# A fused linear attention and MLP kernel: one more block of 512 tokens, and k projections as full-array products

## The chip, the core and the metric

The kernel runs on one core of a Trainium2 chip. A core has five engines that run side by side and meet only at semaphores: PE (TensorE, the matrix multiplier, which writes to PSUM), DVE (VectorE, elementwise work and reductions), ACT (ScalarE, activation functions and copies), POOL (GpSimd) and SP (SyncE, which here only issues transfers). PEld in the profile is the loading of a matmul's stationary operand. The metric is the device time of one execution in microseconds (us); lower is better.

## What is computed

Linear attention over 8 batches of 576 tokens with 8 heads of 64, followed by a two-layer perceptron over all 4608 tokens:

```python
def phi(x):
    proj = np.einsum('bhsd,df->bhsf', x, w_phi)
    proj = proj - np.max(np.abs(proj), axis=-1, keepdims=True)
    return np.concatenate([np.exp(proj), np.exp(-proj)], axis=-1)

q_p, k_p = phi(q), phi(k)
kv = np.einsum('bhsf,bhsd->bhfd', k_p, v)
z = np.sum(k_p, axis=2)
num = np.einsum('bhsf,bhfd->bhsd', q_p, kv)
den = np.einsum('bhsf,bhf->bhs', q_p, z)[..., None] + 1e-06
x = (num / den)            # tokens x 512
h = x @ w_in               # 512 -> 2048
y = 0.5 * h * (1.0 + erf(h / sqrt(2)))
out = y @ w_out            # 2048 -> 512
```

The features number 128 per sign. The MLP weights arrive in 64-bit floats and are taken apart on the chip.

## The kernel before

**A planner writes the order.** Every piece of work is an `Op` with an engine, an estimated cost, the buffers it reads and writes, and a `rank` (a due time). `Plan.order` (L118) simulates the engines with these estimates and lists the operations: on each engine, among those that can start, the one with the lowest rank goes first. `plan.since` holds operations back until a planned time, `plan.gate` makes them wait for a list of earlier ones. `Plan.emit` writes the instructions in that order; on the chip each engine runs its own list strictly in order. Attention matmuls carry a bonus in rank (`PULL`, L113), so that PE takes them as soon as they are ready; GELU work carries one on ACT and DVE (`URGE`). Matmuls have a `kind`: "f" and "s" use the whole array, "k", "q", "v", "n" and "d" use it in parts, and the planner gathers those into lumps (`LUMP`, `LINGER`, L190) because changing the shape costs time. The constants at the end of the file (L853 to L891) are the due times and thresholds.

**Buffers** are slots of named pools (L298, L300). In PSUM there are `pp` (one slot of two banks), `kv`, `pn`, `po` (two banks) and `ph` (two slots).

**Attention.** `k_quad` (L389) treats four heads of a batch in five units of two or one chunks of 128 tokens: a projection of k into `pk`, DVE's maximum of magnitudes (`mx`) and a subtraction into `ek`, two exponentials on ACT, and matmuls that sum k features times v into `kv`. Each k projection is a pair of fp32 matmuls of 64 rows each, for two heads, into two banks. `q_pair` (L470) treats two heads and half of the tokens: q is rounded and split (`qh`), projected into `pq` by matmuls of the rounded type (fp32r), copied to `pc` on ACT, reduced over the partitions on POOL (`mb`), subtracted on DVE, put through two exponentials (`ef`); then DVE forms `un`, POOL sums it to the denominators (`db`), PE makes the numerators (`pn`), and both go to DRAM (`x_d`, `d_d`). `quotients` (L558) takes reciprocals (`r_d`). Batches 0 and 1 use other forms (`b < EB`, `b < ND`): for them k projections alternate between `pp` and `po`.

**MLP.** fp32 products are made of three fp32r products of a rounded part and a remainder. `block` (L589) does 256 tokens: it loads `xr` and `rb`, multiplies, splits into `xh` and `xl`, and for each of eight steps runs 24 first products into `ph`, two GELUs (`gh` and in place), a subtraction (`gl`) and 12 second products into `po`. `wide_block` (L686) does 512 tokens with seven products of quarter matrices in place of eight (`pa`, `pb`), for which `combos` (L657) forms sums of weight quarters beforehand and stores them to DRAM (`s_d`); its second products go to `po` and `pp`. Its outputs leave through `ob` (L809 to L814), two slots. The first 2 x `JW` = 10 blocks are narrow, the other four are wide. `combos` and the wide blocks are gated by the last 60 operations of the attention (L835, L843).

**Queues.** All transfers are issued by SP, in order.

Of the kernel before, what the change touches and what calls it, by code (L numbers as in the profile page):

```python
# [55 lines left out]
class Op:  # L56
    __slots__ = ("eng", "cost", "fn", "bufs", "rank", "table", "late", "deps", "users", "wait", "ready", "start", "end", "n", "names", "nbytes", "duty", "kind", "psum")


class Plan:  # L60
# [30 lines left out]
    def op(self, eng, cost, fn, r=(), w=(), also=(), rank=0.0, table=None, late=0.0, kb=0, duty=1.0, kind="f", psum=False):  # L91
        o = Op()
        o.eng, o.cost, o.fn, o.rank, o.table, o.late, o.n = eng, cost, fn, rank, table, late, len(self.ops)
        o.users, o.ready, o.nbytes, o.duty, o.kind, o.psum = [], self.since, kb, duty, kind, psum
# [23 lines left out]
    def order(self, bias):  # L118
# [56 lines left out]
        while len(done) < n:  # L175
            best = None
            for e, lst in cand.items():
# [12 lines left out]
                if e == "pe" and last[0] == "f":  # L190
                    t_of = {id(o): max(o.ready, first.setdefault(o.n, t)) for t, o in opts}
                    there = [o for t, o in opts if t <= lim and o.kind != "f"]
                    if sum(o.cost for o in there) < LUMP and all(lim - t_of[id(o)] < LINGER for o in there):
                        hold = 4000.0
                key = None
                for t, o in opts:
                    if t <= lim:
# [3 lines left out]
                        if o.kind != "f":  # L201
                            k += hold
# [83 lines left out]
def fused_kernel(ctx: ExitStack, tc: tile.TileContext, qT, kT, va, w_st, w_in, w_out, out):  # L286
# [11 lines left out]
    SLOTS = dict(kt=2, vt=2, mx=2, ek=4, kvn=3, un=1, db=1, qt=1, pc=2, mb=2, ef=2, xo=2, dc=2, rb=1, xr=1, xh=2, xl=2, gh=2, gl=2, ob=2)  # L298
    sb = {t: plan.pool(spool, t, n) for t, n in SLOTS.items()}
    PS = dict(pp=1, kv=1, pn=1, ph=2, po=1)  # L300
# [37 lines left out]


# [49 lines left out]
    def k_quad(b, g, kvs, rank):  # L389
# [18 lines left out]
        for u, (p, cs) in enumerate(units):  # L408
            n = len(cs)
            mx = sb["mx"]([P, 2, 2 * n], F32, f"mx_{nm}_{u}")  # L410
            x = ps[EARLY_PK[turn[0] % len(EARLY_PK)] if b < EB else "pp"]([P, 2, 512], F32, f"pk_{nm}_{u}")
# [8 lines left out]
            xs = lambda x=x, n=n: x()[:, :, : n * NF].rearrange("p j (i f) -> p j i f", i=n)  # L420

            def proj(x=x, cs=cs):
                return [mm(x()[:, j, i * NF : (i + 1) * NF], lhsT=kt()[64 * j : 64 * j + 64, c * P : (c + 1) * P], rhs=wst()[64 * j : 64 * j + 64],
                           start=True, stop=True) for i, c in enumerate(cs) for j in range(2)]

            op("pe", n * PAIR_K, proj, r=[kt, wst], w=[x], also=[mx, *e], kind="k", **k())
            op("dve", dve(256 * n, True), lambda xs=xs, mx=mx: nc.vector.tensor_reduce(  # L427
                out=mx()[:, 0].rearrange("p (j i) -> p j i", j=2), in_=xs(), axis=AX.X, op=ALU.max, apply_absolute_value=True), r=[x], w=[mx], psum=True, **k())
            if b < KB:

                op("dve", 0.09, lambda mx=mx: nc.vector.tensor_scalar(
                    out=mx()[:, 1], in0=mx()[:, 0], scalar1=-1.0, scalar2=None, op0=ALU.mult), r=[mx], w=[mx], **k())
                for s in (1, 0):
                    for j in range(2):
                        for i in range(n):
                            op("act", act(NF, True), lambda xs=xs, es=es, s=s, j=j, i=i, n=n, mx=mx: nc.scalar.activation(
                                es[s]()[:, j, i], xs()[:, j, i], AF.Exp, scale=1.0 - 2.0 * s, bias=mx()[:, 1 - s, j * n + i : j * n + i + 1]),
                               r=[x, mx], w=[e[s]], table="exp", **k())
            else:
                at, of = (es[0], e[0]) if b >= SB else (xs, x)  # L440
                tt("dve", dve(256 * n, True), at, xs, lambda mx=mx, n=n: mx()[:, 0].rearrange("p (j i) -> p j i", j=2).unsqueeze(3).to_broadcast(
                    [P, 2, n, NF]), ALU.subtract, [x, mx], [of], psum=True, **k())
                for s in (1, 0):
                    op("act", act(256 * n, b < SB), lambda at=at, es=es, s=s: nc.scalar.activation(  # L444
                        es[s](), at(), AF.Exp, scale=1.0 - 2.0 * s), r=[of], w=[e[s]], table="exp", **k())
            for pp in (0, 1) if p is None else (p,):
# [6 lines left out]
                for i, c in enumerate(cs):  # L453

                    def sums(acc=acc, rs=rs, c=c, i=i, es=es, first=fresh and i == 0, last=last_u and i == n - 1):
                        ins = []
                        for j in range(2):
                            for s in range(2):
                                for fs in (slice(0, 64), slice(64, P)):
                                    ins.append(mm(  # L460
                                        acc()[fs, 2 * s + j, :], lhsT=es[s]()[rs, j, i, fs], rhs=vt()[rs, 2 * c + j, :],
# [3 lines left out]
                    op("pe", 4 * PAIR_V, sums, r=[*e, vt] + ([] if fresh and i == 0 else [acc]), w=[acc], kind="v", **k())  # L465
# [4 lines left out]
    def q_pair(b, p, kvs, rank, halves=(0, 1)):  # L470
# [4 lines left out]
        for half in halves:  # L475
# [18 lines left out]
            else:  # L494
                pqs = [ps["pp"]([P, 2, 512], F32, f"pq_{nm}")]
                of = [lambda j=j, t=pqs[0]: t()[:, j, :HS] for j in range(2)]
# [4 lines left out]
            else:  # L501
                op("pe", 4 * mm_cost(128, HS), lambda of=of, qh=qh: [
                    mm(of[j](), lhsT=wd()[:, w], rhs=qh()[:, j], start=w == 0, stop=w == 1) for j in range(2) for w in range(2)
                ], r=[qh, wd], w=pqs, also=[pc], kind="s", **k(1))
            if b < EB:
                for j in range(2):
                    copy("act", act(HS, True), lambda pc=pc, j=j: pc()[:, j], of[j], [pqs[j]], [pc], **k(1))
# [423 lines left out]
```

## Time and profile before

| | |
|---|---|
| median of 3 runs | 1128.63 us (1127.2 to 1130.21) |
| profiled execution | 1131.98 us |
| its span, first to last instruction | 1130.2 us |
| PE busy | 1080.8 us (96%) |
| DVE busy | 717.5 us (63%) |
| ACT busy | 626.9 us (55%) |
| POOL busy | 321.0 us (28%) |

"Busy" is the time in which at least one instruction of the engine ran. A row of the timeline gives a start, a length, the engine, the line of the program, the operation, output <- inputs, sizes and a count; in brackets stands the idle time before it and what ended it. Nearly all matmuls have the line of one helper (L305), nearly all DVE operations on two tensors that of another (L331), so groups are told apart by their tiles. A row of the waits reads: who waited, for whom, total us, times, longest.

### The profile page before, as it was taken

The numbers are of one execution on the slowest core, as the hardware profiler recorded it, in microseconds if no ns is written. First come the engines' busy times: TensorE is split into PE (matmuls) and PEld (weight loads), VectorE is DVE, ScalarE is ACT, GpSimd is POOL, SyncE is SP. The second block draws the span as 40 slices with busy tenths as digits, with TensorE's granted clock in tenths as the row PEclk, the third lists the DMA queues.
The fourth block names the chain that finished last, engine by engine and source line by source line (L and its number), as shares of the span: only waits on it lengthen the run. The fifth ranks groups of instructions, "written<-read, shape, count | busy, mean of one in ns | idle before, by whom it ended". The sixth has DMA issues, their size and how long they took to land.

```text
span 1130.2 us, 22251 instructions
## 1 busy us (share of the span) xinstructions
PE 1080.8 (96%) x8904; PEld 908.4 (80%) x8904; DVE 717.5 (63%) x1209; ACT 626.9 (55%) x1023; POOL 321.0 (28%) x116
## 2 busy tenths in 40 slices
PE   7898999999998999999999999999999999899997
PEld 4554878888887887787787888999889898798996
DVE  6989998466787757757877655783535435434331
ACT  5887888776776776678686863222222323222222
POOL 1244223335665454555545452000000000000000
PEclk9999999999999999999999999999999999999999
DMA  9985413123242332332321211665534534534420
GB/s 336 311 305 147 118 36 104 55 75 109 76 117 74 86 93 82 81 98 66 115 90 50 70 33 40 187 183 155 175 113 119 180 113 116 173 94 121 125 82 38
DMA packets 117176, 133.99 MB, mean 119 GB/s; under 512 B 28288, under 2 KB 87840, under 8 KB 117072
## 3 DMA queue, kind: packets, MB, share of 16 engines
q1 hardware_dynamic: 117072, 132.56, 39.1%
q8 instruction: 70, 1.15, 0.4%
q14 instruction: 34, 0.28, 0.1%
HBM read 104.96 MB, written 27.56 MB: 117 GB/s over the span
## 4 chain that ended last, share of the span: by engine, by line
PE 60%; DVE 19%; ACT 7%; DMA 6%; issue 3%; SPq 3%; POOL 2%; DVEq 0%; POOLq 0%; ACTq 0%
PE ph L305 13%; PE po L305 12%; PE po_pp L305 7%; PE pb L305 7%; PE po_po L305 7%; PE pa L305 5%; PE kv L305 3%; PE pn L305 2%; DVE pc L331 2%; DVE mx L427 2%; DVE qh L331 2%; PE pq L305 2%; POOL db L545 2%; PE pk L305 2%; DVE qh L327 1%
## 5 line engine op out<-in xcount | busy, mean ns | idle before, releaser
L305 PE MATMUL ph<-xh,w_i 128*128 128x256 f32 x1280 | 250.6, 284 | 0.0
L545 POOL PARTITION_ALL_REDUCE db<-un x48 | 176.9, 3685 | 165.5 <-DVE un L542 117.1
L305 PEld LDWEIGHTS ph<-xh,w_i 128*128 128x128 f32 x1280 | 206.8, 190 | 6.6 <-issue 1.3
L510 POOL PARTITION_ALL_REDUCE mb<-pc x64 | 146.0, 2286 | 208.8 <-ACT pc L325 188.5
L305 PE MATMUL po<-w_o,gh 128*128 128x512 f32 x640 | 204.4, 401 | 0.0
L305 PE MATMUL ph<-xl,w_i 128*128 128x256 f32 x640 | 182.2, 285 | 0.0
L305 PEld LDWEIGHTS po<-w_o,gh 128*128 128x128 f32 x640 | 113.2, 188 | 26.2 <-issue 3.9
L305 PE MATMUL po<-w_o,gl 128*128 128x512 f32 x320 | 125.8, 393 | 0.0
L305 PEld LDWEIGHTS ph<-xl,w_i 128*128 128x128 f32 x640 | 121.6, 190 | 2.3
L305 PEld LDWEIGHTS kv<-vt,ek 128*64 128x64 f32 (+1 forms) x2560 | 83.9, 137 | 32.4 <-ACT ek L444 10.7
L792 ACT ACTIVATE gh<-pa 128x512 fp32r<-128x512 f32 x32 | 19.1, 598 | 160.0 <-PE po_pp L305 111.6
L305 PE MATMUL pn<-ef,kvn 128*64 128x288 f32 (+1 forms) x512 | 96.9, 424 | 8.8 <-ACT xo L325 8.5
L516 ACT ACTIVATE ef<-pc 128x576 f32<-128x576 f32 x128 | 81.6, 678 | 39.1 <-DVE pc L331 38.7
L305 PE MATMUL kv<-vt,ek 128*64 128x65 f32 (+1 forms) x2560 | 94.4, 225 | 8.1 <-ACT ek L444 5.9
L632 ACT ACTIVATE gh<-ph 128x512 fp32r<-128x512 f32 x80 | 47.9, 598 | 86.0 <-PE ph L305 85.4
L331 DVE TENSOR_TENSOR gl<-ph,gh 128x512 fp32r<-128x512 f32 x80 | 55.0, 687 | 61.2 <-ACT ph L633 60.0
L444 ACT ACTIVATE ek<-ek 128x512 f32<-128x512 f32 (+1 forms) x120 | 70.2, 587 | 32.8 <-DVE ek L331 30.9
L305 PE MATMUL po_pp<-w_o,gh 128*128 128x512 f32 x256 | 80.7, 397 | 4.4 <-ACT ob L325 4.4
L632 ACT ACT_TABLE_LOAD x61 | 78.3, 1283 | 6.3 <-PE ph L305 5.3
L427 DVE TENSOR_REDUCE mx<-pk 128x4 f32<-128x512 f32 (+1 forms) x80 | 50.5, 631 | 48.1 <-PE pk L305 47.9
L305 PE MATMUL po_po<-w_o,gh 128*128 128x512 f32 x256 | 79.8, 393 | 0.0
L305 PE MATMUL pb<-b,s 128*128 128x256 f32 x576 | 79.2, 282 | 0.0
(88 smaller groups left out, 1842.3 us busy)
## 6 DMA issues: line engine op xcount, KB each, us to landing
s<-s_d SPq DMA_DIRECT2D x128, 256.0 KB
qt<-in_qT_dram SPq DMA_DIRECT2D x112, 144.0 KB
vt<-in_va_dram SPq DMA_DIRECT2D x16, 585.0 KB
kt<-in_kT_dram SPq DMA_DIRECT2D x16, 576.0 KB
out_dram<-ob SPq DMA_DIRECT2D x36, 256.0 KB
raw_i<-in_w_in_dram SPq DMA_DIRECT2D x16, 512.0 KB
raw_o<-in_w_out_dram SPq DMA_DIRECT2D x16, 512.0 KB
x_d<-xo SPq DMA_DIRECT2D x48, 144.0 KB
```

Of the source, the lines that this page charges most:

```text
L305: return tc.keep_in_program_order(nc.tensor.matmul(*a, **kw))
L327: op(eng, cost, lambda: e.tensor_copy(out=dst(), in_=src()), r=r, w=w, **kw)
L331: op(eng, cost, lambda: e.tensor_tensor(out=dst(), in0=a(), in1=b(), op=o), r=r, w=w, **kw)
L427: op("dve", dve(256 * n, True), lambda xs=xs, mx=mx: nc.vector.tensor_reduce(out=mx()[:, 0].rearrange("p (j i) -> p j i", j=2), in_=xs(), ...
L444: op("act", act(256 * n, b < SB), lambda at=at, es=es, s=s: nc.scalar.activation(es[s](), at(), AF.Exp, scale=1.0 - 2.0 * s), r=[of], w=[e ...
L510: op("pool", 2.2, lambda mb=mb, pc=pc: nc.gpsimd.partition_all_reduce(mb(), pc(), P, bass_isa.ReduceOp.absmax), r=[pc], w=[mb], **k(1))
L516: op("act", act(2 * HS), lambda ef=ef, pc=pc, s=s: nc.scalar.activation(ef()[:, s], pc(), AF.Exp, scale=1.0 - 2.0 * s), r=[pc], w=[ef], ta ...
L545: op("pool", 3.7, lambda db=db, un=un: nc.gpsimd.partition_all_reduce(db(), un(), P, bass_isa.ReduceOp.add), r=[un], w=[db], **k())
L632: op("act", act(2 * TB, True) + 0.016, lambda gh=gh, ph=ph: nc.scalar.activation(gh(), ph(), AF.Gelu), r=[ph], w=[gh], table="gelu", rank= ...
L792: op("act", act(2 * TB, psum) + 0.016, lambda gh=gh, at=at: nc.scalar.activation(gh(), at(), AF.Gelu), r=[at], w=[gh], table="gelu", rank= ...
```

## The change

- `JW` goes from 5 to 4: eight narrow blocks and five wide ones.
- From batch 2 on, k is split on DVE into a rounded part and a remainder (`kh`, one slot), and a chunk's projections of both heads are three full-array fp32r matmuls of 256 columns against a block-diagonal weight `wbd` (rounded part and remainder). Both heads of a unit lie in one bank.
- `pp` becomes two slots of one bank. A k unit of batch 0 or 1 that used `pp` takes two of them and is reduced and subtracted in halves; q projections take one per head, with a copy on ACT each; a wide block's second output takes both.
- `vt` is loaded in two pieces into half-size slots.
- A wide block's stores are entered after the next block's loads and splits, and the second half of them leaves through `db` and `qt` in place of `ob`; split 6 uses two `vt` slots.
- `combos` is gated by the last 60 operations of the stream "k" in place of the whole attention, and uses `kt` and `vt` in place of `mb` and `pc`.
- The planner treats kind "s" like "f" when it gathers lumps; many constants change.

```diff
-    SLOTS = dict(kt=2, vt=2, mx=2, ek=4, kvn=3, ...)
+    SLOTS = dict(kt=2, vt=2, kh=1, mx=2, ek=4, kvn=3, ...)
-    PS = dict(pp=1, kv=1, pn=1, ph=2, po=1)
+    PS = dict(pp=2, kv=1, pn=1, ph=2, po=1)
...
+    wbd = fixed([P, 2, 2 * NF], F32R, "wbd")
+    op("dve", dve(512, fast=True), lambda: nc.vector.memset(wbd().bitcast(F32), 0.0), w=[wbd], rank=WB)
+    for j in range(2):
+        copy("dve", dve(2 * NF, fast=True), lambda j=j: wbd()[64 * j : 64 * j + 64, :, j * NF : (j + 1) * NF], lambda j=j: wd()[64 * j : 64 * j + 64],
+             [wd, wbd], [wbd], rank=WB)
...
+            if way == "full":
+                kh = sb["kh"]([P, 2, n * P], F32R, f"kh_{nm}_{u}")
+                copy("dve", dve(n * P, fast=True), lambda kh=kh: kh()[:, 0], lambda cols=cols: kt()[:, cols], [kts[u]], [kh], also=[kt], **k())
+                tt("dve", dve(n * P), lambda kh=kh: kh()[:, 1], lambda cols=cols: kt()[:, cols], lambda kh=kh: kh()[:, 0].bitcast(F32), ALU.subtract,
+                   [kts[u], kh], [kh], also=[kt], **k())
+
+                def proj(xb=xb, cs=cs, kh=kh):
+                    ins = []
+                    for i, c in enumerate(cs):
+                        at = slice(i * 2 * NF, (i + 1) * 2 * NF)
+                        for z, w in ((0, 0), (0, 1), (1, 0)):
+                            ins.append(mm(xb[0]()[:, at], lhsT=kh()[:, z, i * P : (i + 1) * P],
+                                          rhs=wbd()[:, w], start=len(ins) % 3 == 0, stop=len(ins) % 3 == 2))
+                    return ins
+
+                op("pe", 3 * n * mm_cost(128, 2 * NF), proj, r=[kh, wbd], w=xb, also=[mx, *e], kind="s", **k())
...
-                pqs = [ps["pp"]([P, 2, 512], F32, f"pq_{nm}")]
+                pqs = [ps["pp"]([P, HS], F32, f"pq_{nm}_{j}") for j in range(2)]
...
-                copy("act", act(2 * HS, True), pc, lambda t=pqs[0]: t()[:, :, :HS], pqs, [pc], **k(1))
+            for j in range(2):
+                copy("act", act(HS, True), lambda pc=pc, j=j: pc()[:, j], of[j], [pqs[j]], [pc], **k(1))
...
+        while after:
+            after.pop()()
+        po0 = ps["po"]([P, 2, DM], F32, f"po_{j}")
+        po1 = [ps["pp"]([P, DM], F32, f"po_{j}_{m}") for m in range(2)]
...
+        def stores():
+            for t in range(2):
+                for m in range(2):
+                    ob = sb["ob" if t == 0 else ("db", "qt")[m]]([P, DM], F32, f"ob_{j}_{t}_{m}")
+                    copy("act", act(DM, True), ob, po[t][m][1], [po[t][m][0]], [ob], rank=rank(1))
+                    row = t0 + t * TB + m * P
+                    op("sp", 0.06, lambda row=row, ob=ob: nc.sync.dma_start(out=out[row : row + P, :], in_=ob()), r=[ob], kb=262, rank=rank(1))
+
+        after.append(stores)
...
-    plan.gate = gate
+    plan.gate = [o for o in plan.ops if o.stream == "k"][-GATE:]
     combos(lambda x: T0 + CR + CSPAN * x)
...
-JW = 5
+WB = 0.0
+JW = 4
-T15 = 947.637
+T15 = 960.04
-HOLD2 = 0.0
+HOLD2 = 24.49
-TF = 76.044
+TF = 87.606
-LUMP = 1.066
-LINGER = 2.713
+LUMP = 2.465
+LINGER = 2.039
-LEAD = 320.754
+LEAD = 367.572
-T0 = 50.594
+T0 = 87.078
```

More of the change, by code (lines that the diff above doesn't have):

```diff
@@ L56 @@
 class Op:
-    __slots__ = ("eng", "cost", "fn", "bufs", "rank", "table", "late", "deps", "users", "wait", "ready", "start", "end", "n", "names", "nbytes", "duty", "kind", "psum")
+    __slots__ = ("eng", "cost", "fn", "bufs", "rank", "table", "late", "deps", "users", "wait", "ready", "start", "end", "n", "names", "nbytes", "duty", "kind", "psum", "stream")
 class Plan:
@@ L189, in order @@
                 hold = 0.0
-                if e == "pe" and last[0] == "f":
+                if e == "pe" and last[0] in "fs":
                     t_of = {id(o): max(o.ready, first.setdefault(o.n, t)) for t, o in opts}
-                    there = [o for t, o in opts if t <= lim and o.kind != "f"]
+                    there = [o for t, o in opts if t <= lim and o.kind not in "fs"]
                     if sum(o.cost for o in there) < LUMP and all(lim - t_of[id(o)] < LINGER for o in there):
@@ L419, in k_quad @@
             turn[0] += 1
[L420 to L428, printed above, removed]
@@ new lines, in k_quad, with proj @@
+            cols = slice(cs[0] * P, (cs[-1] + 1) * P)
+            if way == "full":
[12 more added lines that the diff above has]
+                op("pe", 3 * n * mm_cost(128, 2 * NF), proj, r=[kh, wbd], w=xb, also=[mx, *e], kind="s", **k())
+            else:
+                def proj(xj=xj, cs=cs):
+                    return [mm(xj[j]()[:, i * NF : (i + 1) * NF], lhsT=kt()[64 * j : 64 * j + 64, c * P : (c + 1) * P], rhs=wst()[64 * j : 64 * j + 64],
+                               start=True, stop=True) for i, c in enumerate(cs) for j in range(2)]
+                op("pe", n * PAIR_K, proj, r=[kts[u], wst], w=xb, also=[kt, mx, *e], kind="k", **k())
@@ new lines, in k_quad @@
+            inside = way == "po"
+            for x, view, js in parts:
+                nj = js.stop - js.start
+                op("dve", dve(128 * n * nj, True), lambda view=view, mx=mx, js=js: nc.vector.tensor_reduce(
+                    out=mx()[:, 0].rearrange("p (j i) -> p j i", j=2)[:, js], in_=view(), axis=AX.X, op=ALU.max, apply_absolute_value=True),
+                   r=[x], w=[mx], psum=True, **k())
+                at = view if inside else (lambda es=es, js=js: es[0]()[:, js])
+                tt("dve", dve(128 * n * nj, True), at, view, lambda mx=mx, n=n, js=js, nj=nj: mx()[:, 0].rearrange("p (j i) -> p j i", j=2)[:, js].unsqueeze(3).to_broadcast(
+                    [P, nj, n, NF]), ALU.subtract, [x, mx], [x if inside else e[0]], psum=True, **k())
@@ L446, in k_quad @@
+            for s in (1, 0):
+                at = parts[0][1] if inside else es[0]
+                op("act", act(256 * n, inside), lambda at=at, es=es, s=s: nc.scalar.activation(
+                    es[s](), at(), AF.Exp, scale=1.0 - 2.0 * s), r=[parts[0][0] if inside else e[0]], w=[e[s]], table="exp", **k())
             for pp in (0, 1) if p is None else (p,):
@@ L494, in q_pair @@
             else:
-                pqs = [ps["pp"]([P, 2, 512], F32, f"pq_{nm}")]
-                of = [lambda j=j, t=pqs[0]: t()[:, j, :HS] for j in range(2)]
+                pqs = [ps["pp"]([P, HS], F32, f"pq_{nm}_{j}") for j in range(2)]
+                of = [lambda t=t: t() for t in pqs]
             if b < EB:
@@ L762, in go @@
                         for w, x in ((0, 0), (0, 1), (1, 0)):
-                            ins.append(mm(bank()[:, z], lhsT=a(i, w), rhs=bs[n]()[:, x, i], start=first and not ins, stop=len(ins) == 5,
+                            ins.append(mm(bank()[:, z], lhsT=a(i, w), rhs=bs[n][0][x]()[:, i], start=first and not ins, stop=len(ins) == 5,
                                           skip_group_check=True))
                     return ins
-                op("pe", 6 * mm_cost(128, TB), go, r=[*r, bs[n]], w=[bank], rank=rank((u - AHEADW) / NU))
+                op("pe", 6 * mm_cost(128, TB), go, r=[*r, *bs[n][1]], w=[bank], rank=rank((u - AHEADW) / NU))
             uu = sb["kvn"]([P, TB], F32, f"u2_{j}_{u}")
@@ L845, in fused_kernel @@
         wide_block(j, lambda x, t=T0 + 2 * j * d: t + 2 * d * x)
+    while after:
+        after.pop()()
     plan.gate = []
```

101 lines of the change are left out of this document (50 added, 51 removed).

## The prediction

> **What bounds the kernel now.** I read the page's busy table and forty slices first, then the same by stage.
>
> ```profile
> PE 1080.8 (96%) x8904; PEld 908.4 (80%) x8904; DVE 717.5 (63%) x1209; ACT 626.9 (55%) x1023; POOL 321.0 (28%) x116
> PE   7898999999998999999999999999999999899997
> DVE  6989998466787757757877655783535435434331
> ```
>
> PE, at 96%, has nearly no free time; DVE looks idle only because its work stands in the first two thirds. The windows by stage (columns: stretch, length, then busy us of PE, PEld, DVE, ACT, POOL) show it:
>
> ```profile
> 0.00:110.00 110.00, 91.58 (x1093) 56.41 (x1094) 93.36 (x155) 81.42 (x181) 36.29 (x20) 0.98 0.84 279
> 110.00:200.00 90.00, 86.10 (x758) 72.26 (x756) 84.71 (x148) 74.82 (x114) 22.85 (x8) 0.98 0.31 88
> 200.00:440.00 240.00, 233.61 (x2153) 195.36 (x2151) 163.69 (x243) 172.83 (x251) 127.40 (x44) 0.99 0.30 85
> 440.00:690.00 250.00, 241.21 (x2235) 200.00 (x2234) 170.15 (x252) 182.51 (x266) 130.91 (x45) 1.00 0.25 73
> 690.00:778.00 88.00, 88.00 (x570) 80.09 (x570) 60.88 (x122) 19.38 (x37) 3.59 (x1) 1.00 0.58 167
> 778.00:1125.00 347.00, 340.31 (x2104) 304.26 (x2102) 144.68 (x293) 94.78 (x175) 0.00 (x0) 1.00 0.40 119
> ```
>
> From 110 to 778 PE idles 3.9 + 6.4 + 8.8 + 0 = 19.1 us of 668 (2.9%), and DVE works 84.7 + 163.7 + 170.2 + 60.9 = 479.5 us (72%). Three rows of the timeline mark the borders, the last attention matmuls (`pn`) among them:
>
> ```profile
> 110.60 0.50 PE L305 MATMUL ph<-xh,w_i 128*128 128x256 f32 x1
> 687.67 1.19 PE L305 MATMUL pn<-ef,kvn 128*64 128x288 f32 x8
> 778.65 0.88 PE L305 MATMUL pa<-b,w_i 128*128 128x256 f32 x6
> ```
>
> So 0 to 110 is start-up, 110 to 689 narrow blocks mixed with attention, 689 to 778.65 narrow blocks alone, then four wide blocks. What PE waits for between 98 and 700, and in the whole trace:
>
> ```profile
> PE pq L305 <- DVE ek L331: 7.9, 11, 1.2
> PE pk L305 <- DVE ek L331: 4.2, 4, 2.0
> PE pk L305 <- ACT pc L325: 1.5, 1, 1.5
> ...
> PE po_pp L305 <- ACT ob L325: 4.4, 2, 3.0
> ```
>
> The first three are one thing: the only two-bank slot `pp` is held until DVE (or ACT) has read the projection before. They are 7.9 + 4.2 + 1.5 = 13.6 us of the 19.1.
>
> **The change part by part**, against the profiled execution: 1131.98 us with a span of 1130.2, so 1.8 outside it; it stands 3.35 above the median of 1128.63.
>
> 1. **A fifth wide block.** The chain of work over narrow blocks alone gives the pace:
>
> ```profile
> 725.50 2.85 PE ph L305 x24
> 728.35 2.76 PE po L305 x12
> 731.11 2.80 PE ph L305 x24
> ```
>
> 24 first products of 256 columns take 2.85 us (0.119 each), 12 second products of 512 columns 2.76 (0.230). A narrow block has 192 and 96: 22.8 + 22.1 = 44.9 us. A wide block has 8 x 7 x 6 = 336 and 192: 40.0 + 44.2 = 84.2, against 89.8 for two narrow: **-5.7 us**. Check: 4 x 84.2 = 336.8 against 345.7 from 778.65 to 1124.3.
>
> 2. **Stores of the wide blocks.** At a block's end four copies leave `po` and `pp` through two `ob` slots, so the third waits until a store has landed:
>
> ```profile
> 965.07 0.58 ACT L325 COPY ob<-po_pp 128x512 f32<-128x512 f32 x1 [7.40 <-DMA out_dram<-ob]
> 967.28 1.08 PE L305 MATMUL po_pp<-w_o,gh 128*128 128x512 f32 x2 [3.01 <-ACT ob L325]
> 971.03 0.63 PE L305 MATMUL po_pp<-w_o,gh 128*128 128x512 f32 x2
> ```
>
> PE loses 4.4 us in two such waits, and after the longer one it ran at half pace: nine matmuls take 971.03 - 967.28 = 3.75 us where 9 x 0.230 = 2.1 is due, so 1.7 more. With `db` and `qt` there are four targets. But those two free only after DVE has multiplied the next block's second half, and SP now holds the stores behind that block's loads: a late load becomes the same wait. Bounds 0 and -6.1; I take **-5**, since these loads no longer stand behind two waiting stores.
>
> 3. **K projections.** Timeline rows of one two-chunk unit:
>
> ```profile
> 511.31 0.71 PE L305 MATMUL pk<-wst,kt 64*128 64x128 f32 x8
> 511.96 0.74 PE L305 MATMUL po<-w_o,gh 128*128 128x512 f32 x2
> 512.53 0.40 PE L305 MATMUL po<-w_o,gl 128*128 128x512 f32 x1
> 512.77 0.63 PE L305 MATMUL po<-w_o,gh 128*128 128x512 f32 x2
> ```
>
> The unit takes 0.65 us to the next start, and the pair behind it 0.74 in place of 0.63. New: six full-array matmuls of 256 columns, 6 x 0.119 = 0.71, and no change of shape. A unit alone between FFN work gains 0.05; one beside `kv` or `pn`, which pay the change anyway, loses 0.06. Over 48 such units and 12 of half the size, +-3 us; I take **0**. [...]
>
> 4. **Their price on DVE.** Each later unit now needs a cast and a subtraction of `kt` before PE can start, through one `kh` slot. Nearest rows (tile view: min/median/max ns; lines view: mean):
>
> ```profile
> L327 DVE CAST qh<-qt x48: 397/648/2749, 108.1 to 668.7; 128x576 fp32r<-128x576 f32 x48
> L331 DVE TENSOR_TENSOR qh<-qt,qh x48: 754/756/1850, 109.9 to 669.7; 64x576 fp32r<-64x576 f32 x48
> L331 DVE TENSOR_TENSOR qh<-qt,qh 64x576 fp32r<-64x576 f32 x48 | 47.3, 985 | 1.6
> L327 DVE CAST qh<-qt 128x576 fp32r<-128x576 f32 x48 | 42.9, 894 | 8.7 <-DMA qt<-in_qT_dram 7.9 <-PE pq L305 0.7
> L331 DVE TENSOR_TENSOR c<-u,pb 128x256 f32<-128x256 f32 x64 | 26.7, 417 | 1.1
> ```
>
> Low: 0.397 x 256/576 = 0.18, and 0.42: 0.59 a unit (half for the small ones), 32 us in all. High: adding what the mean exceeds the minimum by, 0.50 for the cast and 0.23 for the subtraction, 1.3 and 1.0 a unit: 75 us. I take the middle, 53. [...]
>
> DVE from 110 to the wide stage: 479.5, less two narrow blocks' preparation and `gl`:
>
> ```profile
> L331 DVE TENSOR_TENSOR gl<-ph,gh 128x512 fp32r<-128x512 f32 x80 | 55.0, 687 | 61.2 <-ACT ph L633 60.0 <-PE pn L305 0.9
> L331 DVE TENSOR_TENSOR xr<-xr,rb 128x1024 f32<-128x1024 f32 x10 | 15.1, 1515 | 11.2 <-DMA d_d<-db 4.0 <-DMA xr<-x_d 3.8 <-DMA rb<-r_d 2.2
> L327 DVE CAST xh<-xr 128x1024 fp32r<-128x1024 f32 x10 | 13.9, 1392 | 8.0 <-PE ph L305 8.0
> L331 DVE TENSOR_TENSOR xl<-xr,xh 128x1024 fp32r<-128x1024 f32 x10 | 12.2, 1220 | 0.1
> ```
>
> (55.0 + 15.1 + 13.9 + 12.2) / 10 = 9.6 each, so 479.5 - 19.2 + 53 = 513, in a stretch that PE would cut to 668 - 90 = 578: 89% in place of 72%. The one stretch with DVE that full is 110 to 200 (94%), where PE idles 3.9 of 90, 4.3%. Over 578 that is 25 us, against 19.1 now: +5.9.
>
> 5. **Two one-bank slots** let a projection run while the one before is read. Of the 13.6 us above I give back half, -6.8 (bounds 0 and -13.6), since with DVE fuller the reader comes later too. With part 4: **-1**. The q copy is cut in two on ACT:
>
> ```profile
> L325 ACT COPY pc<-pq 128x576 f32<-128x576 f32 x48 | 30.5, 636 | 14.5 <-PE pq L305 14.4
> L325 ACT COPY pc<-pq 128x288 f32<-128x288 f32 x32 | 11.6, 405 | 0.4 <-PE pq L305 0.3
> ```
>
> 2 x 405 - 636 = 174 ns, 8.4 us over 48, under PE's work on an ACT busy 355 of 490 us; uncovered, it lengthens each q chain by 0.17.
>
> 6. **Start-up and order.** The FFN is released in the plan at 87.6 in place of 76.0, but its first matmul came at 110.6 anyway: 0, at most +11.6 if the lag stays. Early `pp` units read in halves: ten of twenty units with four instructions for two, some 3 us on a DVE busy 93 of 110; **+1** for PE. The weight `wbd` costs DVE a memset and two copies, under a microsecond, in the same +1. What happens at the border, by the timeline of the first wide block:
>
> ```profile
> 780.15 2.03 SPq L702 DMA_DIRECT2D xr<-x_d  x4
> 790.53 0.69 DVE L331 TENSOR_TENSOR xr<-xr,rp 128x512 f32<-128x512 f32 x1 [1.88 <-DMA rp<-r_d]
> ```
>
> Four load issues take SP 2.03 us, 0.5 each; `vt` in two pieces adds 16 of them, 8 us spread over SP's queue, with `qt`, `xr` and the stores behind; nothing of it on PE's path while the loads run ahead. The combination sums move from behind the attention's last operations to behind its last `k` operations; their DVE work stands inside the 479.5 before and after, and cost PE nothing in the 88 us where it ran (88.00 busy of 88.00). The wide loads stay behind the attention's last 60 operations, with narrow matmuls as cover: **+1** for a cover grown thinner.
>
> **Sum**: -5.7 - 5 + 0 - 1 + 1 + 1 = -9.7: 1122.3 in this execution, 1119 against the median.
>
> **Rivals.**
>
> *The attention keeps its pace.* Now two narrow blocks (778.65 - 688.8 = 89.9 us) remain when it ends; the change takes exactly those away. For: PE prefers attention work whenever it is ready, so its pace is that of its chain, not of a due time. If it ends at 689 again, the loads and first split follow uncovered, about 12 us: 10.4 from the first load to the multiplication in the rows above, and one split. Then 701 + 421 (five blocks) + 1.6 (left-over waits) + 5.9 (tail) + 1.8 - 3.35 = 1128: no change.
>
> *DVE becomes the bound (slower).* Before the first wide product it must do 572.8 (0 to 778) - 19.2 + 3 + the splits. At the share of 0 to 200, (93.36 + 84.71) / 200 = 89%, splits of 53 give 610 / 0.89 = 685, level with PE; splits of 75 give 632 / 0.89 = 710, so 710 + 421 + 1.6 + 5.9 + 1.8 - 3.35 = 1137. It decides from about 68 us of splits, or a DVE share below 87%. [...]
>
> *All slot waits go and the splits are hidden.* -5.7 - 6.1 - 13.6 - 3 = -28: 1100. Against: DVE has still to read every projection.
>
> **How the numbers follow.** Forecast 0.54, attention pace 0.14, DVE bound 0.22, everything gained 0.10. A measurement can tell about 0.3% (3.4 us) from no change: faster 0.64, same 0.14, slower 0.22. The range runs from the third rival's end, 1101, to the second's, 1136.
>
> **What would show it.** Right: 48 fewer first products; `pq` and `pk` waiting for DVE `ek` under 7 us; no wait of `po_pp` for `ob`; `kh` rows of 30 to 75 us; last `pn` before 680 and the first wide product near 690. Wrong: PE idle for several us between the last narrow and the first wide matmul, or `pk` waiting for `kh`.

## The result, and the profile after

The changed kernel takes 1144.44 us (median of 4 runs, 1143.34 to 1144.62), the kernel before, timed beside it, 1129.3. The ratio is 1.0129, 95% interval 1.0113 to 1.0146: **slower by 15 us**, where 1119 was forecast in a range of 1101 to 1136. Its profiled execution took 1143.34 us with a span of 1141.6, against 1131.98 and 1130.2 before. The difference of the spans, 11.4 us, is what the traces explain below; the medians lie 15.1 apart, and the other 3.7 us stand in no trace.

From the page after:

```profile
PE 1082.1 (95%) x8748; PEld 913.1 (80%) x8748; DVE 783.4 (69%) x1408; ACT 614.3 (54%) x1063; POOL 329.2 (29%) x116
PE   7878999999989999999999999999999999999998
DVE  6999999879889869887788976535435434525332
```

156 matmuls fewer, yet PE is busy 1.3 us longer; DVE has 66 us more, and mostly 8s and 9s stand where mostly 5s to 8s stood in the first half. The windows by stage (columns as before):

```profile
0.00:117.00 117.00, 93.95 (x1071) 58.99 (x1071) 104.99 (x200) 89.04 (x190) 37.05 (x20) 0.97 0.75 256
117.00:200.00 83.00, 80.16 (x634) 68.08 (x633) 80.28 (x139) 69.58 (x107) 26.45 (x9) 1.00 0.30 82
200.00:440.00 240.00, 226.65 (x2222) 188.48 (x2221) 203.84 (x330) 174.12 (x283) 139.93 (x47) 1.00 0.33 93
440.00:650.00 210.00, 203.62 (x1875) 171.84 (x1874) 172.40 (x291) 151.56 (x243) 116.60 (x39) 0.99 0.30 87
650.00:693.00 43.00, 43.00 (x273) 38.75 (x273) 30.47 (x66) 9.78 (x18) 9.14 (x2) 1.00 0.69 194
693.00:1138.00 445.00, 434.76 (x2681) 386.99 (x2680) 191.47 (x387) 120.15 (x224) 0.00 (x0) 0.99 0.41 126
```

From 200 to 440 DVE is busy 85% in place of 68%, and PE's idle time there has doubled, 6.4 to 13.4 us. In the wide stage PE idles 10.2 (6.7 before). The borders, from PE's timeline of the changed kernel (first MLP product, last `pn`, first wide product, last matmul):

```profile
117.84 0.38 PE L305 MATMUL ph<-xh,w_i 128*128 128x256 f32 x1
...
647.19 1.19 PE L305 MATMUL pn<-ef,kvn 128*64 128x288 f32 x8
...
693.42 0.88 PE L305 MATMUL pa<-b,w_i 128*128 128x256 f32 x6
...
1137.00 0.40 PE L305 MATMUL po<-w_o,gl 128*128 128x512 f32 x1
```

The attention now ends 40 us earlier in the narrow stage, but the wide products start only 85.2 us earlier than the row at 778.65. The same border needs care, because wide and narrow products mix there. In the kernel before, wide products begin sooner than the row that the prediction took:

```profile
770.18 1.59 PE L305 MATMUL pb<-b,s 128*128 128x256 f32 x12
```

So I count in work. Border = start of the first wide product, plus the narrow products still to come after it at 0.119 and 0.230 us. Before: 770.18 + 24 x 0.119 + 24 x 0.230 = 778.55. After: 693.42 + 12 x 0.119 + 24 x 0.230 = 700.4. What the wide stage takes beyond 84.2 us a block is its excess. Last matmul end before: 1124.4.

| | before | after | difference | forecast |
|---|---|---|---|---|
| border, less the 89.8 us of two narrow blocks | 688.75 | 700.4 | +11.6 | +1 |
| wide blocks at 84.2 | 336.8 | 421.0 | with the 89.8: -5.6 | -5.7 |
| excess of the wide stage | 9.1 | 16.0 | +6.9 | -5 |
| tail, last matmul to the end of the span | 5.8 | 4.2 | -1.6 | 0 |
| sum | | | +11.3 | -9.7 |

The sum meets the 11.4 us of the spans. One saving came as counted; two losses have to be explained. The loss at the border has three parts. PE idles 4.1 us more before 120 us (23.0 in place of 18.9: 120 less the busy time in the rows below, of the kernel before, the changed kernel and run e6, which comes later). It idles 4.0 more from there to the first wide product (22.6 in place of 18.6). And it is busy 3.5 us longer for what lies ahead of the border.

```profile
0.00:120.00 120.00, 101.07 (x1177) 63.28 (x1178) 103.29 (x171) 88.81 (x194) 36.29 (x20) 0.99 0.80 265
0.00:120.00 120.00, 96.95 (x1105) 61.70 (x1106) 107.99 (x207) 90.65 (x193) 37.05 (x20) 0.97 0.74 250
0.00:120.00 120.00, 97.14 (x1110) 62.19 (x1111) 108.06 (x203) 91.46 (x195) 36.96 (x20) 0.97 0.74 250
```

What PE waits for in the changed kernel from 98 to 693, and from 690 to 1140 (who, for whom: total us, times, longest):

```profile
PE pq L305 <- DVE qh L331: 8.2, 7, 3.3
PE pq L305 <- DVE ek L331: 4.0, 5, 1.2
PE pn L305 <- ACT xo L325: 3.2, 6, 1.3
PE pk L305 <- DVE kh L331: 3.1, 3, 1.5
PE pk L305 <- DVE kh L327: 1.9, 4, 0.7
PE pk L305 <- ACT pc L325: 1.5, 2, 1.1
...
PE pk L305 <- DVE ek L331: 0.8, 1, 0.8
PE pq L305 <- ACT pc L325: 0.7, 1, 0.7
```
```profile
PE pa L305 <- DVE u L331: 7.2, 4, 2.4
PE pa L305 <- DVE gl L331: 2.4, 1, 2.4
```

The waits for a slot fell as the prediction said: `ek` and `pc` from 13.6 to 4.0 + 1.5 + 0.8 + 0.7 = 7.0. In their place stand waits for DVE's splits: those of k (`kh`), 5.0, and those of q (`qh`), up from 2.8 to 8.2. `po_pp` for `ob` is gone from the wide stage, and `pa` waits for `u` instead.

### The profile page after: what moved, and what is told of

Its sections match the earlier page's. It is cut to its first block, busy times and chain, and to the rows that moved or that the text cites. A ratio compares the mean times of both kernels' runs of the same rounds, so it can differ in the third digit from the quotient of the medians.

```text
span 1141.6 us, 22352 instructions
## 1 busy us (share of the span) xinstructions
PE 1082.1 (95%) x8748; PEld 913.1 (80%) x8748; DVE 783.4 (69%) x1408; ACT 614.3 (54%) x1063; POOL 329.2 (29%) x116
## 4 chain that ended last, share of the span: by engine, by line
PE 56%; DVE 20%; DMA 8%; ACT 6%; issue 5%; SPq 3%; POOL 2%; DVEq 0%; ACTq 0%; POOLq 0%
PE po L305 24%; PE pb L305 9%; PE ph L305 7%; PE pa L305 7%; PE pn L305 3%; PE kv L305 2%; DVE qh L331 2%; PE pk L305 2%; DVE qh L327 2%; DVE mx L469 2%; DVE gl L331 2%; DVE kh L327 1%; DMA rp<-r_d 1%; POOL db L576 1%; PE pq L305 1%
## 5 line engine op out<-in xcount | busy, mean ns | idle before, releaser
L305 PE MATMUL po<-w_o,gh 128*128 128x512 f32 x1152 | 366.1, 399 | 0.0
L305 PEld LDWEIGHTS po<-w_o,gh 128*128 128x128 f32 x1152 | 205.8, 190 | 39.7 <-issue 3.9
L305 PE MATMUL po<-w_o,gl 128*128 128x512 f32 x576 | 228.1, 396 | 0.0
L305 PE MATMUL ph<-xh,w_i 128*128 128x256 f32 x1024 | 198.0, 281 | 0.0
L305 PEld LDWEIGHTS ph<-xh,w_i 128*128 128x128 f32 x1024 | 163.9, 188 | 3.6 <-issue 1.3
L305 PE MATMUL ph<-xl,w_i 128*128 128x256 f32 x512 | 144.7, 283 | 0.0
L305 PEld LDWEIGHTS po<-w_o,gl 128*128 128x128 f32 x576 | 109.1, 189 | 26.6 <-DVE gl L331 0.4
L305 PE MATMUL kv<-vt,ek 128*64 128x65 f32 (+1 forms) x2560 | 96.0, 227 | 11.9 <-ACT ek L477 10.4
L305 PEld LDWEIGHTS pb<-b,s 128*128 128x128 f32 x720 | 91.9, 190 | 1.4 <-DVE c L331 0.6
L305 PEld LDWEIGHTS pa<-b,w_i 128*128 128x128 f32 x480 | 67.5, 190 | 18.5 <-DVE u L331 9.2
L305 PE MATMUL pa<-b,w_i 128*128 128x256 f32 x480 | 70.8, 283 | 9.6 <-DVE u L331 7.2
```

What stands on the lines that cost most here:

```text
L305: return tc.keep_in_program_order(nc.tensor.matmul(*a, **kw))
```

## Two theories of the wide stage

**Theory:** the stores were moved out of one wait into another. Timeline of the changed kernel just after the end of a wide block (rows of PE's matmuls in between left out):

```profile
883.87 0.45 SPq L858 DMA_DIRECT2D out_dram<-ob  x1
...
888.25 2.53 SPq L738 DMA_DIRECT2D rp<-r_d  x4
...
891.51 8.12 SPq L738 DMA_DIRECT2D rp<-r_d  x12
...
893.43 0.69 DVE L331 TENSOR_TENSOR xr<-xr,rp 128x512 f32<-128x512 f32 x1 [5.36 <-DMA rp<-r_d]
894.04 0.69 DVE L331 TENSOR_TENSOR gl<-pa,gh 128x512 fp32r<-128x512 f32 x1
...
896.39 0.69 DVE L331 TENSOR_TENSOR xr<-xr,rp 128x512 f32<-128x512 f32 x1 [1.66 <-issue]
...
897.33 0.68 DVE L331 TENSOR_TENSOR gl<-c,gh 128x512 fp32r<-128x512 f32 x1
897.93 0.42 DVE L331 TENSOR_TENSOR u<-u,pa 128x256 f32<-128x256 f32 x1
...
898.40 1.65 PE L305 MATMUL pa<-b,w_i 128*128 128x256 f32 x6 [2.42 <-DVE u L331]
```

Read it upwards. PE waits for `u`; `u` stands in DVE's list behind two multiplications `xr<-xr,rp` for the next block, which PE does not need yet. The first of them waits 5.36 us for the loads `rp`, and these go into `db` and `qt`, from which the last store was issued at 883.87 and has to land first (888.25; the issuing queue waits 3.4 us for it). For the 1.66 us before the second, the row names no cause ("issue"); that loads hold it too is inferred from the twelve that SP is issuing from 891.51 on. **Rival:** the slots are innocent; the planner simply thinks that these loads land sooner than they do and puts the multiplication too early.

**e1** gives the second pair of stores slots of its own (room of `kh` and `wbd`, idle by then). **e2** lets `rp` count 4 us later in the plan. **e3** does both.

```diff
# e1
+    sb["wb"] = plan.pool(spool, "wb", 1)
-    wbd = fixed([P, 2, 2 * NF], F32R, "wbd")
+    wbd = plan.pool(spool, "wb", 1)([P, 2, 2 * NF], F32R, "wbd")
-                    ob = sb["ob" if t == 0 else ("db", "qt")[m]](...)
+                    ob = sb["ob" if t == 0 else ("kh", "wb")[m]](...)
# e2
-                o.late = dma[0] + 0.15 - o.end
+                o.late += dma[0] + 0.15 - o.end
-                           r=[r_d[b][h]], w=[rp[z]], also=[x], kb=n * 0.512, **k)
+                           r=[r_d[b][h]], w=[rp[z]], also=[x], kb=n * 0.512, late=4.0, **k)
```

> The changed kernel with the third and fourth store of a wide block in slots of their own, idle by then (kh and the weight wbd's), in place of db and qt; the order of all engines is the same as in the changed kernel until DVE reaches the first border between wide blocks. Theory 1 (a store held in db and qt keeps the next block's loads of rp back, DVE stops in order at the multiplication, and PE waits for u behind it): the three PE waits for u near 809, 896 and 984 (1.9 to 2.4 us each, two of them followed by half clock) go, and the time falls by 6 to 10 us, to 1134 to 1138. Theory 2 (the loads are late by themselves: sixteen broadcasts in a row, planned to land sooner than they do): the waits stay at 1 us or more at each border and the time falls by less than 3 us, to 1141 or more.

> The changed kernel, with the planner told that each load of rp lands 4 us later than it reckons; slots as in the changed kernel. Order is the same until the last narrow block. Theory 1: the loads still wait for the stores, but DVE gets the multiplications later in its list, so most of the waits for u go: 4 to 8 us faster, 1136 to 1140. Theory 2: the same or more, up to 10 us, 1134. If neither, and the waits for u are only a sign of DVE being full in this stage (DVE is busy 43% there), the time stays within 2 us of 1144.

> Both edits. Theory 1: as e1_own_slots within 2 us, 1134 to 1138. Theory 2: as e2_late_rp. PE from the first wide product to its last one in place of 444 us: 428 (421 of wide work and 7 of narrow work left over) plus at most 4.

| | us (range) | ratio to before, interval | border | excess |
|---|---|---|---|---|
| changed kernel | 1144.44 | 1.0129 [1.0113, 1.0146] | +11.6 | 16.0 |
| e1 own slots | 1141.56 (1139.67 to 1142.4) | 1.0103 [1.0084, 1.0122] | +11.8 | 13.4 |
| e2 later loads | 1139.74 (1136.29 to 1139.83) | 1.0082 [1.0063, 1.0102] | +14.4 | 9.5 |
| e3 both | 1137.93 (1136.91 to 1139.2) | 1.0074 [1.0059, 1.009] | +13.9 | 9.5 |

Border and excess are worked out as above, each from one trace, to some 0.3 us. Own slots alone take half of the waits for `u` (7.2 to 3.9); later loads take all of them. In time the three runs are not clearly apart, since their intervals overlap; the waits tell them apart. So the rival holds more of it: the order in which DVE was told to work made the wait, the landing of the stores made it longer. The first row is what e1 has left; the other three, 4.2 us, are what e3 has left, all of them at the first wide block, where the splits `b` now come late:

```profile
PE pa L306 <- DVE u L332: 3.9, 4, 1.7
...
PE pa L306 <- DVE b L328: 2.9, 1, 2.9
PE pa L306 <- DVE gl L332: 0.7, 1, 0.7
PE pa L306 <- DVE b L332: 0.6, 1, 0.6
```

Both edits together are worth 6.5 us of 15. More than half of the loss lies ahead of the wide stage.

## The k splits

The price that the prediction left widest, by groups and by tile (min/median/max ns), in the changed kernel:

```profile
L327 DVE CAST kh<-kt 128x256 fp32r<-128x256 f32 (+1 forms) x60 | 40.6, 676 | 0.3
L331 DVE TENSOR_TENSOR kh<-kt,kh 128x256 fp32r<-128x256 f32 (+1 forms) x60 | 32.6, 543 | 0.7
```
```profile
L327 DVE CAST kh<-kt x60: 165/290/2669, 74.8 to 607.2; 128x256 fp32r<-128x256 f32 x48, 128x128 fp32r<-128x128 f32 x12
L331 DVE TENSOR_TENSOR kh<-kt,kh x60: 275/416/2726, 76.8 to 610.1; 128x256 fp32r<-128x256 f32 x48, 128x128 fp32r<-128x128 f32 x12
```

73.2 us: the high end of the forecast's 32 to 75, not the 53 that it took. The subtraction's median, 0.42, is that of the low end, and the cast's, 0.29, lies above its 0.18. The means, 0.68 and 0.54, come near those of the high end (0.68 and 0.65), since some instructions take over 2 us: in the timeline, the 13 casts and 5 subtractions that take over 1 us lie wholly within all-reduces on POOL. **Theory:** these splits are most of what the border lost. **Rival:** it lost by the later start (first MLP product at 117.84 in place of 110.60), the halves of the early units, or the new order.

**e5** leaves out the subtraction, so that the remainder's product uses the rounded part (a wide block's first products also use the rounded weight part where the remainder stands). **e6** leaves out both split operations; the products read a constant tile of zeros, and PE no longer waits for a split. In both the lists of the other engines are as in the changed kernel.

```diff
# e5
-                tt("dve", dve(n * P), lambda kh=kh: kh()[:, 1], ..., ALU.subtract, [kts[u], kh], [kh], also=[kt], **k())
+                op("dve", dve(n * P), lambda: [], r=[kts[u], kh], w=[kh], also=[kt], **k())
# e6, in addition
-                copy("dve", dve(n * P, fast=True), lambda kh=kh: kh()[:, 0], ..., [kts[u]], [kh], also=[kt], **k())
+                op("dve", dve(n * P, fast=True), lambda: [], r=[kts[u]], w=[kh], also=[kt], **k())
-                            ins.append(mm(xb[0]()[:, at], lhsT=kh()[:, z, i * P : (i + 1) * P],
+                            ins.append(mm(xb[0]()[:, at], lhsT=khfix()[:, z, i * P : (i + 1) * P],
```

> The changed kernel without the subtraction that makes the remainder of k (60 DVE instructions, 32.6 us); the third product uses the rounded part again, so PE, ACT, POOL and SP have the very same lists. The remainder of k is left out. If the splits' DVE time is what the stretch before the wide blocks loses, about half of the loss comes back: the first wide product at 686 to 690 in place of 693.4, and the time 3 to 7 us lower, 1137 to 1141. If DVE's fullness is harmless there (PE waits only where the list is badly ordered), less than 2 us.

> The changed kernel without the cast and the subtraction of k (120 DVE instructions, 73.2 us); the products read one constant tile in place of k, all other lists as they are. The k projections are left out as a result. Theory of the splits: PE's waits for kh (5.0 us) go and those for qh (8.2) fall to about the 2.8 of before; first wide product at 680 to 685, time 8 to 13 us lower, 1131 to 1136. Rival (start-up and order): first MLP product still at 116 or later and the time at most 5 us lower.

e5: 1135.31 us (1133.25 to 1137.19), ratio 1.0052 [1.0038, 1.0066]. e6: 1132.08 (1129.51 to 1135.8), 1.0027 [1.0013, 1.0041]. **The splits cost 12.4 of the 15 us** by the medians (11.5 by the ratios); the subtraction alone is 9.1, more than the 3 to 7 expected. In the traced execution of e6, the fastest of its ten, the border is at +1.3 in place of +11.6. That still holds the late start: the first MLP product comes at 117.3, and PE idles 22.9 us before 120, as the third of the rows above shows, 3.9 more than before. Afterwards it idles 3.1 less than before (15.5 in place of 18.6) and is busy 0.5 longer. So some 4 us of the border are the start-up's, and ahead of the wide stage the splits cost 10.3, which hid a gain of the other parts. The page of e6:

```profile
PE 1077.0 (95%) x8748; PEld 910.7 (81%) x8748; DVE 734.4 (65%) x1289; ACT 614.3 (54%) x1063; POOL 327.0 (29%) x116
```

DVE's busy time falls by 49.0 us, not by 73.2: neighbouring rows overlap (in the rows of the changed kernel above, one of 0.68 us at 897.33 runs past the next start, 897.93), and other groups grow when `kh` is gone (`un<-ef,kvn` 40.5 to 45.6, `qh` 49.4 to 52.3, `pc` 58.2 to 60.5). So part of the long `kh` rows seems to be waiting that some DVE instruction does anyway. And PE's same 8748 matmuls take 5.1 us less, on top of the idle time, at the same mean granted clock (0.993 and 0.992).

Two things in e6 speak against a simple account. PE's waits for `qh`, expected to fall to 2.8, stay; there DVE's cast of q waits 14.4 us for its loads, where it waits 5.7 in the changed kernel:

```profile
PE pq L305 <- DVE qh L331: 9.2, 8, 3.0
L327 DVE CAST qh<-qt 128x576 fp32r<-128x576 f32 x48 | 37.7, 785 | 14.5 <-DMA qt<-in_qT_dram 14.4
```

So the time that the k splits take does not explain the growth of the `qh` waits. And the excess of the wide stage is 11.8 in place of 16.0, though no k is split there and the order is the same; how the waits at the block ends come to be shorter was not followed up.

**e12** puts the cast on ACT (on top of e3), which has room: busy 54%.

```diff
-                copy("dve", dve(n * P, fast=True), lambda kh=kh: kh()[:, 0], ...
+                copy("act", act(n * P), lambda kh=kh: kh()[:, 0], ...
```

> e3_own_and_late (1137.9) with the cast of k on ACT in place of DVE: 40.6 us off DVE, some 23 us more on ACT (60 at 0.28 to 0.4). The plan is made anew. Theory of DVE's price: 1130 to 1135. Rival: ACT, busy 73% in the mixed stage, passes the delay on through the exponentials and GELUs: 1137 or more.

1148.78 (1145.41 to 1149.1), 1.0181 [1.0158, 1.0205], slower than e3. The long casts are gone:

```profile
L326 ACT CAST kh<-kt x60: 281/404/417, 74.8 to 624.4; 128x256 fp32r<-128x256 f32 x48, 128x128 fp32r<-128x128 f32 x12
```

but the planner wrote another order for it, in which the attention ends at 677 and PE waits 18.6 us for `b`, the split of the first wide block. So e12 leaves open what a cast on ACT is worth in the same order. That wait is the next question.

## The border, and what the fifth block is worth

Five kernels change only the plan or the number of wide blocks. e4: four wide blocks in the changed kernel. e8: five in the kernel before, no other change. e7: the MLP released in the plan as early as before. e9: k projections as before (fp32 pairs) in the changed kernel. e13: the changed kernel with the planner's constants of before.

```diff
# e4
-JW = 4
+JW = 5
# e8, on the kernel before
-JW = 5
+JW = 4
# e7
-TF = 87.606
+TF = 77.0
# e9
-            way = EARLY_PK[turn[0] % len(EARLY_PK)] if b < EB else "full"
+            way = EARLY_PK[turn[0] % len(EARLY_PK)] if b < EB else "pp"
# e13: T15, PATIENCE, WPACE, WSPAN, HOLD2, TF, LUMP, LINGER, LEAD, HOLD, WR, ATR, T0 as before
```

> The changed kernel with JW = 5 again: ten narrow and four wide blocks, all else as changed. If the fifth wide block is worth what was forecast (5.7 us of products less, paid with one more border between wide blocks, 3 us), the time rises by 2 to 6 us, to 1146 to 1150. Rival: the fifth block is itself the loss, because the attention has to be done 90 us sooner and narrow cover is gone at the border: then the time falls by 5 us or more, to 1139 or less.

> The kernel before with JW = 4 and nothing else: eight narrow and five wide blocks, old k projections, old slots, combination sums still behind the whole attention. By the forecast's terms PE does 5.7 us less. If the attention keeps its end at 689 and the sums (40 us of DVE) and loads follow uncovered, PE stands idle for 20 to 40 us before the first wide product: 1145 to 1165. If the planner finds cover, 1122 to 1128.

> The changed kernel with the MLP released in the plan at 77.0 in place of 87.6 (before: 76.0); the order changes from the start-up on. If the release holds the MLP back, its first product comes near 108 to 111 in place of 117.8, and 4 to 8 us of it are left at the end: 1136 to 1140. Rival: DVE is full until 200 in either case, PE loses there what it gains here: first product earlier, but the time within 3 us of 1144.

> The changed kernel with the k projections of batch 2 and on as fp32 pairs again, into the two one-bank slots (each half reduced and subtracted by itself, some 0.3 us more of DVE a unit, 18 us); no kh. The plan is made anew. If DVE time is the price, 73 - 18 = 55 us of DVE less give back three quarters of the 12.4 us that e6_no_split gave: 1133 to 1138. Rival: the pairs take both slots at once, so the waits that the two slots removed come back (13.6 us before) and changes of shape with them: 1141 or more.

> The changed kernel with the planner's constants of before (due times, LUMP, LINGER, TF). The order of the attention changes. If the constants are a small matter, it stays within 4 us of the changed kernel: 1140 to 1149. If with five wide blocks the end of the attention decides, a last pn after 665 uncovers the first wide block's loads and splits: PE then waits 10 to 30 us for b before the first wide product, and the time is 1150 to 1175. If the new constants cost what the change loses, it falls to 1125 to 1135, with the first MLP product near 110.

| | us (range) | ratio, interval | last `pn` ends near | PE's waits for `b` |
|---|---|---|---|---|
| changed kernel | 1144.44 | 1.0129 [1.0113, 1.0146] | 648 | 0 |
| e4 four wide | 1138.76 (1137.6 to 1142.94) | 1.0088 [1.0065, 1.0111] | 672 | 0 |
| e7 | 1149.81 (1147.21 to 1151.36) | 1.0174 [1.0142, 1.0205] | 675 | 14.2 |
| e9 | 1166.48 (1162.02 to 1171.78) | 1.035 [1.0314, 1.0385] | 669 | 29.9 |
| e13 | 1181.36 (1180.96 to 1182.18) | 1.0473 [1.0448, 1.0498] | 710 | 26.2 |
| e8 before, five wide | 1203.77 (1202.48 to 1207.26) | 1.0662 [1.0633, 1.0691] | 687 | 16.1 |

With five wide blocks, each of these plans whose attention ends at 669 or later leaves PE without narrow work while the first wide block's loads and split run, as in e9:

```profile
717.29 1.22 PE L305 MATMUL pa<-b,w_i 128*128 128x256 f32 x2 [24.84 <-DVE b L327]
```

This is the first rival of the prediction as a mechanism. The changed kernel escapes it, because its order ends the attention at 648 and keeps a whole narrow block as cover. e8 has besides a wait of 58.9 us of `pa` for the loads of the weight sums, which come behind the old gate:

```profile
PE pa L305 <- DMA s<-s_d: 58.9, 1, 58.9
```

e13, the change without its new constants, is 37 us slower than with them, so they are not where the time was lost. That the fifth block needs the moved `combos` as well is suggested by e8's wait; no run tried it alone. The expectations of e7, e8, e13 and, below, e14 missed: each of these edits makes the planner write another order, and no expectation foresaw it.

e4 says what the fifth block brought here: it is 5.7 us *faster* to leave it out. Its excess is 6.4 us for four wide blocks against 16.0 for five, its border +9.6 against +11.6. So the arithmetic saving of 5.6 is there, and more than that goes into waits (its order is planned anew, so the 5.7 is not the price of one block alone).

**Is it the splits or the rest?** e10 is e9 with e3's two edits and four wide blocks: no splits, no fifth block. e11 is the same with the new k projections. e14 is e10 with the constants of before.

> The changed kernel with the old k projections, ten narrow and four wide blocks, own slots for the stores and the later planned rp: what is left of the change are the one-bank slots, the deferred stores and the constants. By the sum: before, less some of the 13.6 us of slot waits and 6 to 8 us of waits in the wide stage: 1118 to 1126, faster than both kernels. If start-up and constants cost 7 us by themselves (first MLP product at 117 in place of 110), 1127 to 1133.

> e4_four_wide with own slots and the later planned rp, new k projections. Its wide stage had 5.3 us of waits: 1134 to 1137, if the splits' price of some 10 us stays. Against e10 it shows that price with four wide blocks.

> The kernel of run e10 (k projections as before, four wide blocks, stores in slots of their own, later loads) with the constants of before. If the late start (first MLP product at 120 in place of 110) is what keeps e10 level with before, the first MLP product comes at 110 to 113 and the time is 1120 to 1125. If that start only moves work, the time stays at 1126 to 1134.

| | us (range) | ratio, interval | border | excess |
|---|---|---|---|---|
| e10 old k | 1129.93 (1125.46 to 1133.79) | 1.0009 [0.9989, 1.003] | +7.7 | 0.9 |
| e11 new k | 1134.53 (1132.24 to 1134.68) | 1.006 [1.0043, 1.0077] | +9.8 | 0.9 |
| e14 old k, old constants | 1138.18 (1136.21 to 1140.82) | 1.0097 [1.0064, 1.013] | +14.0 | 0.7 |

The new k projections cost 4.6 us here too; the orders differ, so this is no clean price. e14's first MLP product comes at 107.8, e10's at 120.4, and e14 is 8 us slower: an earlier first product does not make the kernel faster by itself. e10 has 8 us less excess than the kernel before and is only level with it, since its border is 7.7 late. Its waits from 98 to 700 show one gain that is missing:

```profile
PE pq L306 <- DVE ek L332: 13.1, 15, 3.1
```

An old k unit takes both one-bank slots, so the slot waits stay at 13.1 (13.6 before). So the halved slot brings nothing here without the one-bank k projection; the reverse was not tried. Of the 7.7, 1.9 are idle time of PE (3.7 more before 120, less afterwards) and 5.8 longer busy time. These weren't separated further; the halved early units are a candidate.

## A version faster than both

If the wide stage's waits are a matter of order and slots, the kernel before has them too (excess 9.1) and can lose them without a fifth block. **e15** is the kernel before with the later `rp`; **e16** adds two store slots, for which `vt` in two pieces (as in the change, with split 6 in two `vt` slots) makes room.

```diff
# e15 and e16: as e2
# e16, on the kernel before
-    SLOTS = dict(..., gl=2, ob=2)
+    SLOTS = dict(..., gl=2, ob=2, oc=2)
-                ob = sb["ob"]([P, DM], F32, f"ob_{j}_{t}_{m}")
+                ob = sb["oc" if t else "ob"]([P, DM], F32, f"ob_{j}_{t}_{m}")
```

> The kernel before with one edit: the loads rp of the wide blocks count 4 us later in the plan, so that urgent work goes first. The order until the wide stage is the same. The wait of pa for u (1.45 us) goes, the waits of po_pp for ob (4.4 us) and the half pace behind them (1.7) stay: 1 to 2 us faster, 1127 to 1128. If the later loads take over as a new wait of b, it is 2 to 4 us slower.

> The kernel before with vt in two pieces (which frees room), two store slots of their own for a wide block's second pair of outputs, and rp 4 us later in the plan. If the wide stage of before loses what its waits show (4.4 + 1.45 + 1.7), 1121 to 1124 as long as the attention keeps its pace (last pn 685 to 690). If the vt pieces disturb the attention's order, its end moves by several us and the time with it: 1128 to 1136.

e15: 1126.88 (1123.65 to 1131.17), 0.9985 [0.9966, 1.0003], not clearly different from before. **e16: 1124.06 (1122.83 to 1126.52), 0.996 [0.9946, 0.9975]**: 5 us faster than the kernel before, some 20 faster than the changed one. Its wide stage, as a window (columns as above):

```profile
781.00:1118.00 337.00, 337.00 (x2102) 302.09 (x2100) 143.64 (x292) 94.37 (x175) 0.00 (x0) 1.00 0.40 122
```

PE is busy every moment of it; the excess is 0.6, the border 2.4 late. Of the 8.9 us that the prediction saw beyond 336.8, nearly all is gone, without the change's main parts. The slots without the later loads were not tried.

## Why the prediction was wrong

1. **Fifth wide block, -5.7: right** in products (-5.6). That the kernel gains by it was wrong: e4, in an order of its own, is faster without it.
2. **Stores, -5: wrong, measured +6.9 in excess, -1.6 in the tail.** The prediction wrote that "a late load becomes the same wait" and set the bounds at 0 and -6.1. That excluded a loss without a reason. It looked at who frees `db` and `qt`, and not at what stands behind the waiting multiplication in DVE's list: `gl` and `u`, for which PE waits at once. e1 took half of the waits for `u` away, e2 and e3 all. A fifth block also adds one more block end.
3. **K projections on PE, 0: right as far as the traces tell.** A two-chunk unit between MLP products mostly takes 0.70 to 0.72 us to the next start, as counted, and 0.79 to 0.82 behind `kv`. With the same 324 products, e6 is busy only 0.5 us longer than the kernel before ahead of the border.
4. **Splits, with the slots: -1 forecast; this is the step that failed most.** e6 puts the splits at 12.4 us where +5.9 was taken. The busy time was mis-sized, 73.2 for 53 (net 49.0 on DVE). And the conversion left something out: it priced PE's idle time alone. That was 2.8 + 13.4 + 6.4 = 22.6 us from 117 to 693, where the two parts made 19.1 + 5.9 - 6.8 = 18.2. Between the traces of e6 and the changed kernel lie 13.9 us, 8.8 of PE's idle time and 5.1 of its busy time (the same matmuls take longer). What makes them longer is not shown; that they run slower behind waits, as the six behind the wait that ends at 898.40 do (1.65 us in place of 0.88), is the author's estimate. The prediction had counted such longer matmuls, 1.7 us, in part 2 and not here.
5. **One-bank slots, -6.8: right** (13.6 to 7.0, -6.6), with some luck, as half of the waits was only the middle between none and all. e10 shows that they need the one-bank k projection.
6. **Start-up, +1: too small.** PE idles 4.1 us more in the first 120. The weight `wbd`, put under a microsecond, took DVE 1.06 (a memset of 485 ns, two casts of 286 and 291). The border, forecast with +1, cost no wait for `b` in this order, and 14 to 30 us in e7, e9, e12 and e13. The rows from which the prediction took the first wide block's loads (780.15 and 790.53) are the second block's, since wide products run from 770.18 on. The first block's loads begin at 699.36 and its multiplication at 710.78: 11.4 us in place of 10.4, which changes little.

Of the rivals, "DVE becomes the bound" was nearest: it decided from 68 us of splits, and they took 73.2. Its border, 710, was 10 too late; with only 1.6 us of waits in the wide stage it gave 1137, short of 1144, because no case let both losses happen together.

Most of the signs that were to show the prediction right came true all the same: slot waits for `ek` of 4.8 us, no wait of `po_pp` for `ob`, `kh` rows of 73.2, a last `pn` at 647 and a first wide product at 693. They were signs of its mechanism's gains, and none of them measured a loss. Of the signs of being wrong one came: `pk` waits for `kh`.

The splits that took over 1 us lie within all-reduces on POOL. In the changed kernel the subtraction took 275 to 2726 ns, its five longest (1.31 to 2.73 us) among these; the cast took 165 to 2669 ns on DVE and, in e12, 281 to 417 on ACT. The prediction's high end, 75 us, took in long rows by the means of `qh`; the 73.2 come near it.

## What to carry to other kernels

When a transfer's slot is changed, ask what is queued behind the instruction that will wait for the new one, on its engine, and whether that is more urgent; a planner that believes the load is early puts work that cannot start yet in front of urgent work. Price split work on DVE by the mean of like rows, the long ones included (here 676 and 543 ns), not by their minimum (165 and 275), and count the time of PE's matmuls as well as its idle time (here 5.1 us of 13.9). Before adding work to shorten a stage, take that stage's waits away: here that gained 5 us, where the change hoped for 10 and lost 15.

## What was not expected of the hardware

After a wait of 2.42 us that ends at 898.40 the matmuls run at half pace: the granted clock is 0.50 in the next 2.6 us and 0.87 in the 3.0 us after them. Windows of the changed kernel (stretch, length, PE busy, granted clock, DMA share, GB/s) around this wait:

```profile
896.00:898.40 2.40, 0.00 (x0) 0.99 0.29 82
898.40:901.00 2.60, 2.60 (x9) 0.50 0.45 109
901.00:904.00 3.00, 3.00 (x19) 0.87 0.67 221
```

Six matmuls take 1.65 us in place of 0.88. A wait of the same length did not do it at 700.89, where six take 0.97 us and the granted clock is 1.00 up to 702.90:

```profile
700.89 0.97 PE L305 MATMUL pa<-b,w_i 128*128 128x256 f32 x6 [2.42 <-DVE gl L331]
701.70 0.63 PE L305 MATMUL po<-w_o,gh 128*128 128x512 f32 x2
```

So 2.42 us of PE's idle time was followed by half pace once and not the other time; what decides it is not shown.
